# First feed-forward chunk: weight products placed between gate and value matmuls, silu's table loaded ahead of the second halves, three dummy matmuls fewer in q's last groups

## Chip, cores and metric

One core of one Trainium2 chip. The metric is the device time of one execution in microseconds. The profile's span (first to last instruction) is about 2 us shorter than that time. For the runs of the four jobs below it is known for each execution, to 0.1 us, with the mean granted TensorE clock (the share of the full clock that the core was given).

## The reference

```python
# q, k, v: [4, 6016, 256] float32; tau = 1
qn = q / (norm(q, axis=1) + 1e-6);  kn = k / (norm(k, axis=1) + 1e-6)
a = softmax(kn.transpose(0, 2, 1) @ qn / tau, axis=-1)      # [4, 256, 256]
x = (v @ a).reshape(24064, 256)
g = x @ w_gate                                              # [256, 1536]
out = (g * sigmoid(g)) * (x @ w_val) @ w_out
```

## The kernel before

It folds the attention matrix into the feed-forward weights once per batch ("weight products": exp-logits times w_gate and w_val, in 12 units) and then streams v through gate, value and output matmuls. A chunk is 512 rows of v; a step of a chunk is 128 of the 1536 feed-forward columns; a unit is a product for 512 columns, which for the first four units is made in two halves (lo, hi). For batch 0 nothing hides the start: q and k are loaded and reduced first. While q's last four groups come in, the kernel puts dummy matmuls (`keep_warm`) between the real ones.

```python
    for g, which, gl in order:               # k's groups, then q's (NQ = 9; sizes 8,8,8,8,4,4,4,2,1)
        ...
        sqs = [first_square(0, t, which, on_dve=(t % 2 == 1)) for t in ts]   # ScalarE / VectorE
        if which == 0:
            for t in ts:
                gemm1_pair(0, t)             # q'k products, L168/L173
            if g == G_COLS:                  # G_COLS = NQ - 4
                first_cols(0)
            if g in (NQ - 4, NQ - 3):
                keep_warm(1)                 # dummy, L404
        for t, sq in zip(ts, sqs):           # column sums, L218, from G_COLS on
            ...
            if G_COLS <= g < NQ - 2:
                keep_warm(NQ - 2 - g)
    first_softmax(0)   # root, exp, row sums; first halves of units 0-3; then:
        #   for u in range(2): wp_unit(b, u, psum_o, "o", hi)   (unit 0 on ScalarE, 1 on VectorE)
        #   nc.scalar.preload_act_table(ACT.Silu)
    ...
        for f in range(FH):                  # steps of a chunk; gi == 0 is the first chunk
            g_ps, v_ps, mv = gv_matmuls(b, ci, f)
            us = range(2 * f + 2, min(2 * f + 4, len(wp_units))) if gi == 0 else ()
            part = hi if f == 0 else full
            for u in us[:1]:
                wp_unit(0, u, psum_o, "o", part, on_dve=True)
            silu = gv_silu(g_ps, mv)
            for u in us[1:]:
                wp_unit(0, u, psum_o, "o", part, on_dve=(f == 0))
            gv_product(f, sv, silu, v_ps, mv)
            ...
```

Of the kernel before, what the change touches and what calls it, by code (L numbers as in the profile page):

```python
# [13 lines left out]
ACT = mybir.ActivationFunctionType  # L14
# [4 lines left out]
def kernel(  # L19
# [11 lines left out]
    nc = tc.nc  # L31
# [42 lines left out]
    psum_o = ctx.enter_context(tc.tile_pool(name="psum_o", bufs=2, space=bass.MemoryType.PSUM))  # L74
    psum_kq = ctx.enter_context(tc.tile_pool(name="psum_kq", bufs=1, space=bass.MemoryType.PSUM))
    psum_m = ctx.enter_context(tc.tile_pool(name="psum_m", bufs=1, space=bass.MemoryType.PSUM))
# [76 lines left out]
    def evacuate_first_v(h):  # L153
        nc.vector.tensor_copy(vt_ready[(0, 0)][:, h, :], state["vt_ps"][:, h, :])
# [43 lines left out]
    def first_row_copy(b):  # L198
        row = work.tile([1, C], FP32, tag="row")
        nc.vector.tensor_copy(row, state[b, "ss", 0][0:1, :])  # L200
        state[b, "row"] = row
# [21 lines left out]
    def first_root(dst, src):  # L223
        nc.scalar.activation(dst, src, ACT.Ln)
        nc.scalar.activation(dst, dst, ACT.Exp, scale=0.5)
# [11 lines left out]
    def first_softmax(b):  # L237
        kq, ink = state[b, "kq"], state[b, "ink"]
        inq = work.tile([P, CH], FP32, tag="inq")
        first_root(inq, state[b, "cols"])  # L240
        s_f = work.tile([P, CH, C], FP32, tag="s_f")
        nc.vector.tensor_mul(s_f[:, 0, :], kq[:, 0, :], ink)
        nc.vector.tensor_scalar_add(inq, in0=inq, scalar1=1e-6)
        nc.vector.reciprocal(inq, inq)
        if inv_tau != 1.0:
            nc.vector.tensor_scalar_mul(inq, in0=inq, scalar1=inv_tau)
        nc.vector.tensor_mul(s_f[:, 1, :], kq[:, 1, :], ink)
        rs = psum_m.tile([P, CH], FP32, tag="misc")
        keep_warm(1)
        row_eps(rs)  # L250
        transpose_first_v()
        keep_warm(2)
        for h in range(CH):
            evacuate_first_v(h)
        exT = attn.tile([P, CH, C], BF16, tag="exT")
        state[b, "exT"] = exT
        for jh in range(CH):
            nc.scalar.activation(exT[:, jh, :], s_f[:, jh, :], ACT.Exp,
                                 scale=inq[:, jh:jh + 1])


        def row_sum(jh):
            for ih in range(CH):
                nc.tensor.matmul(rs[:, ih:ih + 1], exT[:, jh, ih * P:(ih + 1) * P],
                                 ones_bf[:, 0:1], start=False,
                                 stop=(jh == CH - 1), skip_group_check=True)

        units = []
        for u in range(2 * CH):
            unit_ps = psum_gv.tile([P, HW], FP32, tag="gv"[u % 2])  # L270
            units.append(unit_ps)
        row_sum(0)
        wp_matmul(b, 0, 0, units[0], lo)
        wp_matmul(b, 1, 0, units[1], lo)
        wp_matmul(b, 2, 0, units[2], lo)
        row_sum(1)
        finish_rs(b, rs)
        for u, jh in ((0, 1), (1, 1), (2, 1), (3, 0), (3, 1)):
            wp_matmul(b, u, jh, units[u], lo)
        for u in range(4):  # L280
            wp_evacuate(b, u, units[u], lo, u % 2 == 1)
        for u in range(2):
            wp_unit(b, u, psum_o, "o", hi)
        nc.scalar.preload_act_table(ACT.Silu)

    def norm_acc(b, t):
        q_sb, k_sb = qk_tiles[b]
# [88 lines left out]
    def row_eps(rs):  # L376

        nc.tensor.matmul(rs, ones_f[0:1, :], eps[0:1, :], start=True, stop=False,
                         skip_group_check=True)
# [21 lines left out]
    def keep_warm(n):  # L401
        ps = psum_o.tile([P, 2, C], FP32, tag="o")
        for _ in range(n):
            nc.tensor.matmul(ps, ones_bf, warm_bf, start=True, stop=True)  # L404

    wp_units = [(wc, w, ih) for wc in range(NWC) for w in range(2) for ih in range(CH)]

    HW = WP // 2
    full, lo, hi = slice(0, WP), slice(0, HW), slice(HW, WP)
# [8 lines left out]
    def wp_evacuate(b, u, ps, part, on_dve):  # L418
        wc, w, ih = wp_units[u]
        scale = state[b, "smr"][:, ih:ih + 1]  # L420
        cols = slice(wc * WP + part.start, wc * WP + part.stop)
        dst = state[b, "W"][w][:, ih, cols]
        if on_dve:
            nc.vector.tensor_scalar_mul(dst, in0=ps, scalar1=scale)
        else:
            nc.scalar.activation(dst, ps, ACT.Copy, scale=scale)  # L426

    def wp_unit(b, u, pool=psum_m, tag="misc", part=full, on_dve=None):

        ps = pool.tile([P, part.stop - part.start], FP32, tag=tag)  # L430
        for jh in range(CH):
            wp_matmul(b, u, jh, ps, part)
        wp_evacuate(b, u, ps, part, u % 2 == 1 if on_dve is None else on_dve)

    def gv_matmuls(b, ci, f):
        cs, cm = chunks[ci]
        mv = cm * P
        Wg, Wv = state[b, "W"]
        vT = vt_ready[(b, ci)]
        fs = slice(f * P, (f + 1) * P)  # L440
        g_ps = psum_gv.tile([P, CS * P], FP32, tag="g")
        v_ps = psum_gv.tile([P, CS * P], FP32, tag="v")
        for dst, W in ((g_ps, Wg), (v_ps, Wv)):
            for kk in range(CH):
                nc.tensor.matmul(dst[:, :mv], W[:, kk, fs], vT[:, kk, :mv],  # L445
                                 start=(kk == 0), stop=(kk == CH - 1))
        return g_ps, v_ps, mv
# [189 lines left out]
    NG, NQ = len(kgroups), len(qgroups)  # L637
# [15 lines left out]
    G_COLS = NQ - 4  # L653
    T_COLS = qgroups[G_COLS][0] // 2
    for g, which, gl in order:
        gs, gm = gl[g]
        ts = list(range(gs // 2, (gs + gm + 1) // 2))
        if which == 0 and g == NQ - 1:
            continue
        if which == 0 and g == NQ - 2:  # L660

            gs, gm = gl[g + 1]
            ts += range(gs // 2, (gs + gm + 1) // 2)
        if which == 0 and g == G_COLS:
            first_row_copy(0)
        sqs = [first_square(0, t, which, on_dve=(t % 2 == 1)) for t in ts]
        if which == 0:
            for t in ts:
                gemm1_pair(0, t)
            if g == G_COLS:  # L670
                first_cols(0)
            if g in (NQ - 4, NQ - 3):
                keep_warm(1)
        for t, sq in zip(ts, sqs):
            if which == 0 and g >= G_COLS:
                first_col_sums(0, t, sq)
            else:
                first_row_sums(0, t, which, sq, (T_COLS if which == 0 else NP) - 1)
        if which == 0:
            if g == 0:  # L680
                first_norm_k(0)
                nc.vector.tensor_copy(ident, identf)
            elif g <= 4:
                first_inv_k(0, g - 1)

            if G_COLS <= g < NQ - 2:
                keep_warm(NQ - 2 - g)
    first_softmax(0)


    later = {}

    def at_step(n, what, *args):
        later.setdefault(n, []).append((what, args))

    prev = None
    for gi, (b, ci) in enumerate(allc):
        sv = svpool.tile([P, FH, CS * P], BF16, tag="sv")
        for f in range(FH):
            now = gi * FH + f  # L700
            g_ps, v_ps, mv = gv_matmuls(b, ci, f)


            us = range(2 * f + 2, min(2 * f + 4, len(wp_units))) if gi == 0 else ()
            part = hi if f == 0 else full
            for u in us[:1]:
                wp_unit(0, u, psum_o, "o", part, on_dve=True)
            silu = gv_silu(g_ps, mv)
            for u in us[1:]:
                wp_unit(0, u, psum_o, "o", part, on_dve=(f == 0))  # L710
            gv_product(f, sv, silu, v_ps, mv)
            if prev is not None:
                prev.step()
            if b + 1 < B:
                background(b + 1, ci * FH + f)
            if f == 0 and gi + VT_AHEAD < len(allc):
                load_v(*allc[gi + VT_AHEAD])
                at_step(now + 6, transpose_v, *allc[gi + VT_AHEAD])
            for what, args in later.pop(now, ()):
                what(*args)  # L720
        if gi < len(allc) - 2:
            prev = OutColumns(b, ci, sv)
            n0 = (gi + 1) * FH
            for h in range(CH):
                n = n0 + FH // CH * (h + 1) - 1
                at_step(n, prev.copy, h)
                at_step(n + 2, prev.spill, h)
                at_step(n + 5, prev.transpose, h)
            at_step(n0 + 22, prev.store)
        else:  # L730
            prev = OutStage(b, ci, sv)
# [35 lines left out]
```

## Time and profile before

| | before |
|---|---|
| time, median of the first 3 runs | 811.31 us (810.81 to 812.25) |
| span of the profiled run | 809.0 us |
| TensorE busy | 98% |
| first gate matmul of chunk 1 | 38.05 us |
| first output matmul of chunk 2 | 53.28 us |

The prediction shows the lines on which it rests. "Row copy" is VectorE's copy of q's row sums (31.37 us): up to there the two kernels do the same, so its position is the scatter of a run's start. "First output matmul of chunk 2" lies behind everything that the change touches. The stretch between them, 21.91 us, is what the change can shorten.

### The profile page before, as it was taken

The numbers are of one execution on the slowest core, as the hardware profiler recorded it, in microseconds if no ns is written. First come the engines' busy times: TensorE is split into PE (matmuls) and PEld (weight loads), VectorE is DVE, ScalarE is ACT, GpSimd is POOL, SyncE is SP. The second block draws the span as 40 slices with busy tenths as digits, with TensorE's granted clock in tenths as the row PEclk, the third lists the DMA queues.
The fourth block names the chain that finished last, engine by engine and source line by source line (L and its number), as shares of the span: only waits on it lengthen the run. The fifth ranks groups of instructions, "written<-read, shape, count | busy, mean of one in ns | idle before, by whom it ended". The sixth has DMA issues, their size and how long they took to land.

```text
span 809.0 us, 11969 instructions
## 1 busy us (share of the span) xinstructions
PE 793.5 (98%) x3979; PEld 385.0 (48%) x3979; DVE 550.3 (68%) x841; ACT 454.7 (56%) x803; POOL 256.7 (32%) x314
## 2 busy tenths in 40 slices
PE   4999999999999999999999999999999999999998
PEld 2644444444454444444454444444445444444446
DVE  4777887668667888667666787756866665666654
ACT  4566666555556666555555666655555555555553
POOL 4415888422104786422000777720100000000000
PEclk9999999999999999999999999999999999999999
DMA  9995999799887885889997787468647656565443
GB/s 90 144 154 93 172 157 178 138 123 170 168 152 141 143 140 124 168 71 197 142 147 168 140 156 152 120 133 150 146 105 138 132 138 134 140 127 133 113 119 98
DMA packets 202077, 112.34 MB, mean 139 GB/s; under 512 B 149808, under 2 KB 188848, under 8 KB 201264
## 3 DMA queue, kind: packets, MB, share of 16 engines
q1 hardware_dynamic: 183968, 84.51, 44.8%
q0 software_dynamic: 17904, 27.01, 31.6%
q8 instruction: 31, 0.51, 0.3%
q14 instruction: 30, 0.25, 0.1%
q10 hardware_dynamic: 144, 0.07, 0.0%
HBM read 79.04 MB, written 60.43 MB: 172 GB/s over the span
## 4 chain that ended last, share of the span: by engine, by line
PE 96%; DMA 3%; issue 0%; DVE 0%; POOL 0%; POOLq 0%
PE g_ps L445 30%; PE v_ps L445 30%; PE o_new L486 29%; PE ps L414 2%; DMA q_sb<-in_q_dram 2%; PE kq_new L168 2%; PE o_new L539 1%; DMA k_sb<-in_k_dram 1%; PE ps L404 0%; PE last_ps L563 0%; PE ss_new L195 0%; PE kq_new L173 0%; PE unit_ps L414 0%; PE cs L324 0%; POOL k_sb L111 0%
## 5 line engine op out<-in xcount | busy, mean ns | idle before, releaser
L455 DVE TENSOR_TENSOR sv<-silu,v_ps 128x512 bf16<-128x512 bf16 (+1 forms) x576 | 387.3, 673 | 217.2 <-ACT silu L451 215.8
L451 ACT ACTIVATE silu<-g_ps 128x512 bf16<-128x512 f32 (+1 forms) x576 | 339.3, 589 | 294.3 <-PE g_ps L445 261.3
L445 PE MATMUL g_ps<-vT,Wg 128*128 128x512 bf16 (+1 forms) x1128 | 330.7, 375 | 0.0
L445 PE MATMUL v_ps<-vT,Wv 128*128 128x512 bf16 (+1 forms) x1128 | 330.3, 374 | 0.0
L486 PE MATMUL o_new<-sv,w_out_sb 128*128 128x512 bf16 (+1 forms) x1104 | 324.6, 376 | 0.0
L445 PEld LDWEIGHTS <-Wv 128*128 128x128 bf16 x1152 | 112.7, 98 | 130.7 <-ACT Wv L426 0.2
L300 POOL TENSOR_TENSOR acc_new<-acc_new,sq 128x512 f32<-128x512 f32 x135 | 156.2, 1157 | 55.2 <-DVE sq L290 40.7
L486 PEld LDWEIGHTS <-w_out_sb 128*128 128x128 bf16 x1104 | 108.0, 98 | 126.5
L445 PEld LDWEIGHTS <-Wg 128*128 128x128 bf16 x1152 | 109.6, 98 | 122.2
L126 POOL DMA_DIRECT2D vb_new<-in_v_dram x47 | 24.2, 514 | 257.6 <-DMA vT<-vb_new 256.7
L496 DVE COPY pl<-o_new 128x512 uint16<-128x512 uint16 (+1 forms) x92 | 62.6, 680 | 17.2 <-ACT pl L495 16.8
L290 DVE TENSOR_TENSOR sq<-q_sb 128x512 bf16<-128x512 fp8e5 x72 | 66.0, 916 | 0.0
L495 ACT COPY pl<-o_new 128x512 uint16<-128x512 uint16 (+1 forms) x92 | 53.1, 578 | 18.9 <-PE o_new L486 18.7
L291 ACT ACTIVATE sq<-k_sb 128x512 bf16<-128x512 fp8e5 x72 | 44.2, 614 | 0.0
L168 PE MATMUL kq_new<-k_sb,q_sb 128*128 128x512 fp8e5 x184 | 34.8, 313 | 1.6 <-DMA q_sb<-in_q_dram 1.6
L111 POOL DMA_DIRECT2D q_sb<-in_q_dram x45 | 25.3, 563 | 11.9 <-DMA k_sb<-in_k_dram 10.0
L168 PEld LDWEIGHTS <-q_sb 128*128 128x256 fp8e5 x184 | 22.1, 136 | 10.2 <-DMA q_sb<-in_q_dram 2.8
L195 PE MATMUL ss_new<-sq,ones_bf 128*128 128x256 bf16 x83 | 14.8, 336 | 10.9 <-ACT sq L185 10.9
L359 POOL TENSOR_SCALAR den<-th 128x512 f32<-128x512 f32 x3 | 1.8, 615 | 73.1 <-ACT th L358 73.1
L111 POOL DMA_DIRECT2D k_sb<-in_k_dram x42 | 23.0, 548 | 3.1 <-DVE sq L290 1.7
L295 POOL TENSOR_TENSOR acc_new<-sq 128x512 f32<-128x512 bf16 x3 | 3.5, 1151 | 42.5 <-DVE sq L290 42.5
L195 PEld LDWEIGHTS <-ones_bf 128*128 128x128 bf16 x83 | 9.4, 119 | 14.9 <-issue 10.8
(96 smaller groups left out, 214.4 us busy)
## 6 DMA issues: line engine op xcount, KB each, us to landing
rows<-pl SPq DMA_DIRECT2D x86, 256.0 KB, 2.8
out_dram<-ot_new SPq DMA_DIRECT2D x43, 512.0 KB, 3.9
vb_new<-in_v_dram POOLq DMA_DIRECT2D x43, 256.0 KB, 4.9
q_sb<-in_q_dram POOLq DMA_DIRECT2D x36, 128.0 KB, 6.1
k_sb<-in_k_dram POOLq DMA_DIRECT2D x33, 128.0 KB, 7.1
ot_new<-rows SPq DMA_TRANSPOSE x92, 3.7
k_sb<-in_k_dram POOLq DMA_DIRECT2D x5, 256.0 KB, 9.1
rows<-pl SPq DMA_DIRECT2D x6, 192.0 KB, 2.5
```

The source lines that it names most:

```text
L111: nc.gpsimd.dma_start(out=dst[:, gs:gs + gm, :], in_=src[b].rearrange("(p s) c -> p s c", s=NS)[:, gs:gs + gm, :])
L168: nc.tensor.matmul(kq[:, jh, :], q_sb[:, ps:ps + 2, js], k_sb[:, ps:ps + 2, :], start=(t == 0 and jh == 0), stop=last, perf_mode=DR, skip_ ...
L195: nc.tensor.matmul(state[b, "ss", which], ones_bf, sq[:, s, :], start=(t == 0 and s == 0), stop=(t == t_last and s == pm - 1))
L290: nc.vector.tensor_mul(sq[:, :pm, 0, :], q_sb[:, ps:ps + pm, :], q_sb[:, ps:ps + pm, :])
L291: nc.scalar.activation(sq[:, :pm, 1, :], k_sb[:, ps:ps + pm, :], ACT.Square)
L300: nc.gpsimd.tensor_tensor(out=acc, in0=acc, in1=sq[:, s, :, :], op=ALU.add)
L445: nc.tensor.matmul(dst[:, :mv], W[:, kk, fs], vT[:, kk, :mv], start=(kk == 0), stop=(kk == CH - 1))
L451: nc.scalar.activation(silu[:, :mv], g_ps[:, :mv], ACT.Silu)
L455: nc.vector.tensor_mul(sv[:, f, :mv], silu[:, :mv], v_ps[:, :mv])
L486: nc.tensor.matmul(self.o_ps[h][:, :self.mv], w_out_sb[:, f, h * P:(h + 1) * P], self.sv[:, f, :self.mv], start=(f == 0), stop=(f == FH - 1))
L495: nc.scalar.copy(pl[:, 0, :self.mv], halves[:, 0, :self.mv])
L496: nc.vector.tensor_copy(pl[:, 1, :self.mv], halves[:, 1, :self.mv])
```

## The change

Intent: let real weight products fill TensorE where waits were expected, load silu's table earlier, and drop dummies that stand on the chain. The diff is cut: the lines of the old order that it removes stand in the excerpt above.

```diff
-        for u in range(2):
-            wp_unit(b, u, psum_o, "o", hi)
         nc.scalar.preload_act_table(ACT.Silu)
+        for u in range(2):
+            wp_unit(b, u, psum_o, "o", hi, on_dve=True)
...  (gv_matmuls calls between() just ahead of the value matmuls)
-            if g in (NQ - 4, NQ - 3):
+            if g == NQ - 4:
                 keep_warm(1)
...
-            if G_COLS <= g < NQ - 2:
-                keep_warm(NQ - 2 - g)
+            if g == G_COLS:
+                keep_warm(1)
...
+            us = range(2 * f, 2 * f + 2) if gi == 0 and 2 <= f < len(wp_units) // 2 else ()
+            if us:
+                g_ps, v_ps, mv = gv_matmuls(
+                    b, ci, f, lambda: wp_unit(0, us[0], psum_o, "o", on_dve=True))
+            else:
+                g_ps, v_ps, mv = gv_matmuls(b, ci, f)
+            if gi == 0 and f == 0:
+                wp_unit(0, 2, psum_o, "o", hi, on_dve=True)
+                wp_unit(0, 3, psum_m, "misc", hi, on_dve=True)
             silu = gv_silu(g_ps, mv)
+            if us:
+                wp_unit(0, us[1], psum_o, "o", on_dve=False)
```

More of the change, by code (lines that the diff above doesn't have):

```diff
@@ L281, in first_softmax @@
             wp_evacuate(b, u, units[u], lo, u % 2 == 1)
+        nc.scalar.preload_act_table(ACT.Silu)
         for u in range(2):
-            wp_unit(b, u, psum_o, "o", hi)
-        nc.scalar.preload_act_table(ACT.Silu)
+            wp_unit(b, u, psum_o, "o", hi, on_dve=True)
     def norm_acc(b, t):
@@ L433, in wp_unit, with gv_matmuls @@
         wp_evacuate(b, u, ps, part, u % 2 == 1 if on_dve is None else on_dve)
-    def gv_matmuls(b, ci, f):
+    def gv_matmuls(b, ci, f, between=None):
         cs, cm = chunks[ci]
@@ L443, in gv_matmuls @@
         for dst, W in ((g_ps, Wg), (v_ps, Wv)):
+            if between is not None and dst is v_ps:
+                between()
             for kk in range(CH):
@@ L700 @@
             now = gi * FH + f
-            g_ps, v_ps, mv = gv_matmuls(b, ci, f)
-            us = range(2 * f + 2, min(2 * f + 4, len(wp_units))) if gi == 0 else ()
-            part = hi if f == 0 else full
-            for u in us[:1]:
-                wp_unit(0, u, psum_o, "o", part, on_dve=True)
+            us = range(2 * f, 2 * f + 2) if gi == 0 and 2 <= f < len(wp_units) // 2 else ()
[7 more added lines that the diff above has]
+                wp_unit(0, 3, psum_m, "misc", hi, on_dve=True)
             silu = gv_silu(g_ps, mv)
-            for u in us[1:]:
-                wp_unit(0, u, psum_o, "o", part, on_dve=(f == 0))
+            if us:
+                wp_unit(0, us[1], psum_o, "o", on_dve=False)
             gv_product(f, sv, silu, v_ps, mv)
```

## The prediction

> **What bounds the kernel now.** I first read the page: the busy shares and the chain that ended last.
>
> ```profile
> PE 793.5 (98%) x3979; PEld 385.0 (48%) x3979; DVE 550.3 (68%) x841; ACT 454.7 (56%) x803; POOL 256.7 (32%) x314
> PE 96%; DMA 3%; issue 0%; DVE 0%; POOL 0%; POOLq 0%
> ```
>
> The first line gives busy time, share and instruction count; the second is the chain by engine. TensorE is the chain for 96% of the span. Since a busy TensorE need not be at its peak, I also took the start-to-start distance of all matmuls after 42 us. A 128x512 matmul follows the one before by 0.216 us (39.352, 39.568, 39.784 in the trace). In the 767 us from 42.06 on, only one distance exceeds 0.216 by more than 0.03 without an fp8 pair product being there (0.282 at 196.9). So that long stretch has no slack: it takes up no delay and gives none back. The change can only move the moment at which it starts. The whole question is the first 47 us, which I read next, as the chain in time (start, us, what).
>
> ```profile
> 31.84 0.60 PE cols L208 x4
> 32.44 0.32 PE ps L404
> 32.76 0.18 PE cols L218 x8
> 32.94 0.45 PE ps L404 x2
> 33.40 0.44 PE kq_new L168 x4
> 33.83 0.23 PE ps L404
> 34.06 0.18 PE cols L218 x8
> 34.24 0.24 PE ps L404
> 34.48 0.22 PE kq_new L168 x2
> 34.70 0.23 PE kq_new L173 x2
> 34.93 0.13 PE cols L218 x6
> ```
>
> Here L404 is a dummy matmul (keep_warm), whose result nobody reads. Dummies are links of the chain themselves: the real products behind them had their data. The last four groups of q are issued at 14.32, 16.76, 18.88 and 21.34 and take 16.7, 15.8, 14.3 and 12.3 us to land, so they are there at 31.0, 32.6, 33.2 and 33.6 us, but their products start at 31.1, 33.2, 34.3 and 34.5. In this stage TensorE runs late because of its dummies.
>
> Last, the timelines of ScalarE, VectorE and TensorE at the start of the first chunk (start, us, engine, line).
>
> ```profile
> 38.24 0.48 ACT L426 ACTIVATE Wg<-ps,smr 128x256 bf16<-128x256 f32 x1
> 38.74 1.28 ACT L284 ACT_TABLE_LOAD   x1
> 40.03 1.09 ACT L451 ACTIVATE silu<-g_ps 128x512 bf16<-128x512 f32 x2
> ```
> ```profile
> 41.27 0.74 DVE L424 TENSOR_SCALAR Wg<-ps,smr 128x512 bf16<-128x512 f32 x1
> ```
> ```profile
> 41.51 0.59 PE L445 MATMUL v_ps<-vT_new,Wv 128*128 128x512 bf16 x2
> 42.06 1.02 PE L414 MATMUL ps<-w_val_sb,exT 128*128 128x512 bf16 x4
> ```
>
> From 38.05 on TensorE is dense but for one place: the last value matmul of step 2 starts at 41.726, so the next product was due at 41.942, and it starts at 42.064. It waits 0.12 us for VectorE to empty the PSUM tile of the product two before (41.27 + 0.74 = 42.01, plus 0.05 for the semaphore).
>
> **What the Trainium skill says.** "TensorE: Matmul & The Clock Gate", section "Wait — 56ns, not 53.3ns?", gives 215.7 ns between warm matmuls of 512 columns; the trace agrees (0.2155). Its section "What's actually happening" says that the clock falls to half after an idle window and that activity releases it. The trace shows it: from 17.3 to 20.7 us the granted clock is 0.50, after a stretch (13.8 to 17.3) in which TensorE was busy for 1.35 of 3.4 us; the stretches after it, with 2.7 us and more, all have 1.00. "ScalarE: Activation LUTs", section "What ACT_TABLE_LOAD costs", states about 1283 ns for the load plus about 1380 ns of drain; the trace has the 1.28 us, but the first silu starts 0.01 us after it, so I count no drain.
>
> **The change, part by part.**
>
> *Dummies.* The order of instructions on TensorE has three pairs of weight load and dummy fewer: the second of two before the third-last group of q, and one on each side of that group's column sums.
> 1. Without the second dummy at 33.02, the pair products of that group start 0.216 earlier (their landing, 32.57, is past). The group begins at 33.02 rather than 33.24.
> 2. Without the dummy at 33.67, the column sums start when the four products end, 33.46 rather than 33.90: shift 0.44. They need the squares: ScalarE's end at 33.31, VectorE's at 33.35. Just in time.
> 3. The dummy at 34.10 hid a weight load: the next fp8 weights load behind it. Without it, that load (0.11 exposed) stands alone, so it brings 0.216 - 0.11 = 0.11 more, and adding the small steps between them I get 0.57 in all. Products now at 33.75 and 33.96 (landings 33.2, 33.6), last sums at 34.2 (squares: 33.95 and 34.18). All fit.
>
> So the sums' end moves from 34.92 to about 34.35. What follows (root, reciprocal, exp, row sums, first weight products) is a chain of PE, ScalarE and VectorE that moves along, unless a load is late. From issue plus time to landing: v's first chunk 23.86 + 11.0 = 34.9 (needed at 34.96), first gate columns 26.29 + 9.2 = 35.5 (needed 36.1), first value columns 28.71 + 7.5 = 36.2 (needed 36.3), second gate columns 29.97 + 6.9 = 36.87 (needed 36.93); what is needed is the time in the trace of before less 0.57. Four loads land 0.03 to 0.6 us ahead. So 0.57 is nearly the most that removing dummies could ever bring.
>
> *Table load.* ScalarE no longer evacuates the second half of unit 0 (0.48), and loads silu's table right after the first halves: 37.80 to 39.08 with the shift. First silu 39.09 to 39.68, against 40.03 to 40.62; so 0.95 earlier, of which 0.57 is the shift.
>
> *Order in the first chunk.* Step 1 loses its two products (four matmuls of 512 columns, 0.86 us of TensorE), and each later product stands a step later. The matmuls are the same, in another order. The first gate matmul starts at 38.05 - 0.57 = 37.48; five blocks of 0.43 (gate and value of step 0, two half products, gate and value of step 1) come before step 2's gate matmuls, so these are due at 39.64, but need the PSUM tile that the first silu reads until 39.68, plus 0.05: a new wait of 0.10. The product for columns 512 to 1023 follows at 40.17; its weights land at 40.1 (33.51 + 6.6), again just in time. That is what the place between gate and value is for: in the old order, shifted by 0.57, it would have been due at 39.64 and waited 0.5 us. The next product wanting VectorE's evacuation is due at 41.90; VectorE empties its tile at about 41.69 (40.94 + 0.75), so the old wait of 0.12 goes. I followed the later products in the same way to step 5 and found the closest at 0.1 us of margin.
>
> Sum: -0.57 (dummies) - 0.12 (old wait) + 0.10 (new wait) = -0.59 us. 811.31 - 0.59 = 810.7.
>
> **The rivals.**
> - *The loads take the dummies' place.* The weights' landings don't depend on TensorE. For: margins of 0.03 to 0.1 at four of them, so a load that is 0.3 late gives 0.3 back. Against: all land before they are needed in this trace. If it happens, 811.0 to 811.3.
> - *The clock falls.* Fewer dummies could make a window idle enough for half clock. For: the 17.3 us event. Against: the windows that would be touched had 3.35 and 3.40 us of work of 3.4, and the dummies leave a stretch that gets shorter, not emptier; the sums follow one another. If it happened, 3.4 us at half speed would cost about 1.7 us: 812.5.
> - *ScalarE or VectorE becomes the bound of steps 0 to 3.* VectorE takes one more half evacuation (they follow one another at 0.40 us), and the silu wait of 0.10 could be 0.3 if the table load began later. If so, 811.0.
> - *Placing products between gate and value saves several waits.* Against: there was one wait, of 0.12.
>
> **Range and chances.** Even stripping all idle time of TensorE between 28 and 47 us (under 2 us) would be 0.25% of the time, so a gain over 2% (16 us) is out of reach, and the largest loss I can name is about 2 us. What sets the range is scatter: the three runs before spread over 1.4 us, more than the effect. Around 810.7 I take -0.9 and +0.9: 809.8 to 811.6. Faster 0.005, same 0.99, slower 0.005.
>
> **What would show it right or wrong.** Right: TensorE's last column sums end near 34.3 rather than 34.9; the first gate matmul starts near 37.5 rather than 38.05; the table load starts near 37.8; the step-2 gate matmul waits about 0.1 us for silu; no distance above 0.22 us among the 512-wide matmuls from there to step 6; the first output matmul of the second chunk starts near 52.7 instead of 53.28, and everything after keeps that lead. Wrong: a wait of TensorE for a q, v or weight load at 33 to 40 us; a granted clock of 0.5 in a window after 30 us; or a lead at 53 us that is lost later, which would mean that the long stretch had slack that I did not see.

## The result, and the profile after

After: 810.55 us, median of 4 runs (810.38 to 811.19); before, in the same rounds, 811.78 (810.81 to 812.36). The ratio is 0.9987, 95% interval 0.997 to 1.0005: the same, by the 2% measure. Here and below a ratio is the mean time of one kernel's fast runs over that of the other's of the same rounds, so not quite the ratio of the medians. The time fell inside the predicted range (809.8 to 811.6), at 0.15 us from the predicted 810.7. But the two medians differ by 1.2 us, twice what was predicted, and the trace of after shows a smaller gain, 0.48 us at the first output matmul of chunk 2 (52.80 against 53.28), of which 0.17 is only an earlier start (row copy at 31.20). So neither number can be taken as it stands.

The chain in time of the kernel after, where the prediction showed that of before (start, us, what):

```profile
31.67 0.60 PE cols L208 x4
...
32.43 0.35 PE cols L218 x8
32.79 0.04 issue
32.83 0.64 ACT sq L185
33.47 0.05 issue
33.52 0.35 PE cols L218 x8
33.87 0.27 PE kq_new L168 x2
34.14 0.23 PE kq_new L173 x2
34.38 0.20 PE cols L218 x6
```

L404 is a dummy, L218 are the column sums, L168 and L173 the products of q and k. Three dummies are gone, and ScalarE's square of q (L185), which the column sums need, stands in the chain in their place: q's group 6 landed at 32.73 in this run, 0.16 later than in the trace of before, though the run started 0.17 earlier. TensorE now waits for data. Then ScalarE and TensorE at the start of the first chunk:

```profile
37.84 1.28 ACT L282 ACT_TABLE_LOAD   x1
39.13 1.09 ACT L453 ACTIVATE silu<-g_ps 128x512 bf16<-128x512 f32 x2
```
```profile
39.29 0.59 PE L447 MATMUL v_ps<-vT_new,Wv 128*128 128x512 bf16 x2
39.78 0.59 PE L447 MATMUL g_ps<-vT_new,Wg 128*128 128x512 bf16 x2
40.29 0.59 PE L414 MATMUL ps<-w_gate_sb,exT 128*128 128x512 bf16 x2
40.72 0.59 PE L447 MATMUL v_ps<-vT_new,Wv 128*128 128x512 bf16 x2
41.15 0.59 PE L414 MATMUL ps<-w_gate_sb,exT 128*128 128x512 bf16 x2
```

Two matmuls of 512 columns take 0.43 us at full clock. From 39.29 to 39.78 is 0.49: 0.06 of wait for silu (predicted 0.10). From 39.78 to 40.29 is 0.51: 0.08 of wait for the second block of gate weights, which landed at 40.25. After that every block follows at 0.43, and the wait of 0.12 that before had at 41.94 is gone.

### The profile page after: what moved, and what is told of

The parts are those of the page before. It is cut to its first block, busy times and chain, and to the rows that moved or that the text cites. A ratio compares the mean times of both kernels' runs of the same rounds, so it can differ in the third digit from the quotient of the medians.

```text
span 808.5 us, 11893 instructions
## 1 busy us (share of the span) xinstructions
PE 788.9 (98%) x3902; PEld 384.6 (48%) x3976; DVE 550.3 (68%) x842; ACT 454.4 (56%) x802; POOL 256.7 (32%) x314
## 4 chain that ended last, share of the span: by engine, by line
PE 95%; DMA 3%; issue 1%; ACT 0%; DVE 0%; POOL 0%; POOLq 0%
PE g_ps L447 30%; PE v_ps L447 30%; PE o_new L488 29%; PE ps L414 2%; DMA q_sb<-in_q_dram 2%; PE kq_new L168 2%; PE o_new L541 1%; DMA k_sb<-in_k_dram 1%; ACT silu L453 0%; PE last_ps L565 0%; PE ss_new L195 0%; PE unit_ps L414 0%; PE kq_new L173 0%; PE cols L218 0%; ACT pl L497 0%
## 5 line engine op out<-in xcount | busy, mean ns | idle before, releaser
L447 PE MATMUL v_ps<-vT,Wv 128*128 128x512 bf16 (+1 forms) x1107 | 325.9, 374 | 1.2
L447 PE MATMUL g_ps<-vT,Wg 128*128 128x512 bf16 (+1 forms) x1105 | 325.7, 375 | 1.2
L488 PE MATMUL o_new<-sv,w_out_sb 128*128 128x512 bf16 (+1 forms) x1079 | 319.2, 375 | 1.3
L497 ACT COPY pl<-o_new 128x512 uint16<-128x512 uint16 (+1 forms) x92 | 53.1, 577 | 18.9 <-PE o_new L488 17.9
L168 PE MATMUL kq_new<-k_sb,q_sb 128*128 128x512 fp8e5 x184 | 34.5, 312 | 1.7 <-DMA q_sb<-in_q_dram 1.7
L168 PEld LDWEIGHTS <-q_sb 128*128 128x256 fp8e5 x184 | 22.0, 136 | 10.0 <-DMA q_sb<-in_q_dram 2.9
L295 POOL TENSOR_TENSOR acc_new<-sq 128x512 f32<-128x512 bf16 x3 | 3.5, 1153 | 40.9 <-DVE sq L290 40.9
```

The lines of the kernel that those rows point to most:

```text
L168: nc.tensor.matmul(kq[:, jh, :], q_sb[:, ps:ps + 2, js], k_sb[:, ps:ps + 2, :], start=(t == 0 and jh == 0), stop=last, perf_mode=DR, skip_ ...
L447: nc.tensor.matmul(dst[:, :mv], W[:, kk, fs], vT[:, kk, :mv], start=(kk == 0), stop=(kk == CH - 1))
L488: nc.tensor.matmul(self.o_ps[h][:, :self.mv], w_out_sb[:, f, h * P:(h + 1) * P], self.sv[:, f, :self.mv], start=(f == 0), stop=(f == FH - 1))
L497: nc.scalar.copy(pl[:, 0, :self.mv], halves[:, 0, :self.mv])
```

## The experiments

Each job also timed the kernel before beside its kernels. I first give the jobs (they ran on four chips), then count all spans together. "Distance" is from the row copy to the first output matmul of chunk 2, in the one trace of each run.

### First job: the change again, and its parts

**again**: the changed kernel, unaltered.

> The changed kernel unaltered, for a better interval and a second trace. Measure: the distance from VectorE's copy of the q row sums (up to which both kernels are the same) to the first output matmul of the second chunk: 53.28 - 31.37 = 21.91 us before, 52.80 - 31.20 = 21.60 us in the one trace of after. My theory (dummies and order together bring a few tenths of a microsecond, the rest of the measured 1.2 us between the medians is scatter of start and of loads): distance 21.3 to 21.7, timed 0.3 to 0.7 us faster than before. Rival (the trace missed something and the true gain is 1.2 us): over 1.0 us faster with an interval that excludes 0.6.

Measured: 810.51 us (810.17 to 811.24), ratio 0.9989 (0.9977 to 1.0002). The distance was 22.12, longer than before's 21.91, which neither theory had expected. The timeline of TensorE shows why:

```profile
30.75 0.61 PE L195 MATMUL ss_new<-sq,ones_bf 128*128 128x256 bf16 x4
32.24 0.65 PE L168 MATMUL kq_new<-k_sb,q_sb 128*128 128x512 fp8e5 x4 [0.88 <-DMA q_sb<-in_q_dram]
32.82 0.60 PE L208 MATMUL cols<-ones_f,row 1*128 1x1 f32 x4
```

The products of q's group 5 start at 32.24, after 0.88 us of idle time ended by q's load; in the trace of before they start at 31.09. A load here counts its semaphore up by 16, and the products started 0.05 after the sixteenth count: fifteen had come by 31.02, as usual, and the last came at 32.19. The spans of this job fall into two groups: before 808.9 to 809.0 (4 runs) and 809.8 to 810.0 (4 runs), with one at 811.2; again 808.2 to 808.5 (3) and 809.2 to 809.3 (2), its traced run being one of the latter. I call them early and late runs.

**dummies_only**: before, with the dummies edit alone.

```diff
-            if g in (NQ - 4, NQ - 3):
+            if g == NQ - 4:
                 keep_warm(1)
-            if G_COLS <= g < NQ - 2:
-                keep_warm(NQ - 2 - g)
+            if g == G_COLS:
+                keep_warm(1)
```

> The kernel before with only the three dummies taken out. My theory: the first gate matmul moves 0.3 to 0.57 us ahead, but the product of the second block of gate columns is then due at about 39.65 and waits for its weights, which land at 40.1 to 40.25, so nearly all is given back: distance (row copy to first output matmul of chunk 2) 21.7 to 22.0 against 21.91 of before, time within 0.2 us of before. Rival (the dummies are the whole gain and the order is worth nothing): distance 21.3 to 21.6, time 0.3 to 0.6 faster.

Measured: 811.23 us, ratio 0.9994 (0.998 to 1.0007); spans 808.8, 808.8, 808.9, 808.9 and 809.3. The traced run is the last, and late: its distance, 22.17, is that of again's late run (22.12). So in the one late run the dummies alone bring 0.7 (809.3 against 810.0), as the rival said and more (three dummies at 0.22 are 0.65); in early ones 0.15, as my theory said, though no early run was traced to show the wait.

**order_only**: the changed kernel with before's two `keep_warm` conditions put back.

> The changed kernel with its dummies put back as before: order, table load and VectorE's evacuation alone. My theory: the old wait of 0.12 before the value product goes and a wait of about 0.09 for silu comes, so it is worth 0.03 us: distance 21.8 to 21.95, time within 0.2 us of before. Rival (order and table are the gain): distance 21.3 to 21.6.

Measured: 811.91 us, ratio 1.0002 (0.9989 to 1.0014); spans 808.8 (one early run), 809.9, 809.9, 809.9 and 810.2. In late runs the order is worth nothing that the spans show; the one early run is 0.2 below before's 809.0. The trace (late, and with every load after group 5 some 0.4 us later than usual) can't be compared by its distance, 23.16.

**late_table**: after, with unit 0's second half on ScalarE and the table load behind it.

```diff
-        nc.scalar.preload_act_table(ACT.Silu)
         for u in range(2):
-            wp_unit(b, u, psum_o, "o", hi, on_dve=True)
+            wp_unit(b, u, psum_o, "o", hi)
+        nc.scalar.preload_act_table(ACT.Silu)
```

> The changed kernel with unit 0's second half back on ScalarE and silu's table loaded after it. My theory: the first silu ends about 0.4 us later, step 2's gate matmuls wait about 0.5 instead of 0.06 to 0.1 us for the PSUM tile that it reads, and the lead shrinks by about 0.4 us: distance 21.9 to 22.1. Rival (the silu wait is covered by the wait for the second block of gate weights, which ends at 40.3 in any case): the lead shrinks by 0.1 or less.

Measured: 811.56 us, ratio 1.0006 (0.9989 to 1.0023); spans 808.6, 809.2, 809.6 and 812.4, the last (814.56 us) with a mean clock of 0.994 and no trace. The traced run is early, span 808.6 and distance 21.67, against 21.60 and 21.46 in the two early traces of after. The distance missed my range and is near the rival's. But the wait for silu did grow,

```profile
39.05 0.59 PE L447 MATMUL v_ps<-vT_new,Wv 128*128 128x512 bf16 x2
39.94 0.59 PE L447 MATMUL g_ps<-vT_new,Wg 128*128 128x512 bf16 x2 [0.29 <-ACT silu L453]
40.37 0.59 PE L414 MATMUL ps<-w_gate_sb,exT 128*128 128x512 bf16 x2
```

from 39.05 to 39.94 is 0.89, so 0.46 of wait. The product behind it starts at 40.37, where after had it at 40.29; but the two runs are not alike. In this one the weights had landed at 40.02, not 40.25. Without the wait the product was due at 39.91 and could have started at some 40.06 (0.04 after the landing, as in after), so by this estimate the later table load cost 0.3 us here. The distances agree: ScalarE's root comes 0.11 sooner after the row copy than in after_third (3.17 against 3.28), yet the distance is 0.21 longer. My 0.4 was nearer than the rival's 0.1 or less.

### Second job: before's own scatter, and attempts at more

**before_again**: the kernel before, unaltered.

> The kernel before, unaltered. The runs so far have spans in two groups: before 808.9 to 809.0 and 809.8 to 810.0; after 808.2 to 808.6 and 809.2 to 809.3; and the traces of the later group show one of the 16 completion counts of q's group 5 (the fourth-last) arriving 1.2 us after the other fifteen (32.2 against 31.0 us). My theory: an execution is early or late by this straggler, and the change gains 0.5 in early runs and 0.65 to 0.7 in late ones, so the difference of 1.2 between the medians mixes groups. Expect two groups at 809.0 and 809.9 again, and in the trace the first gate matmul at 38.05 with q's group 5 at 31.0, or at about 39.1 with it at 32.2. Rival (the scatter is not from q's group 5): a run of the later group whose group 5 landed at 31.0.

Measured: 811.66 us, ratio to itself 1.0002; spans 808.9, 809.0, 809.2 and 810.1, 810.2. The traced run is early. By luck it matches the first trace of after load for load: row copy at 31.20 in both, group 6 landed at 32.74 and 32.73, the second gate weights at 40.26 and 40.25. Its chain does not run through the dummies at all:

```profile
16.59 16.15 DMA q_sb<-in_q_dram
32.74 0.28 issue
33.02 0.54 POOL vb_new L126
33.56 0.12 issue
33.68 6.58 DMA w_gate_sb<-in_moe_w_gate_dram
40.27 0.04 issue
40.31 1.04 PE ps L414 x4
```

In this trace GpSimd issues v's next chunk and then the second block of gate weights only when a load of q has landed, and the weight product waits for that load. TensorE was ready earlier:

```profile
39.50 0.59 PE L445 MATMUL v_ps<-vT_new,Wv 128*128 128x512 bf16 x2
40.31 1.04 PE L414 MATMUL ps<-w_gate_sb,exT 128*128 128x512 bf16 x4 [0.21 <-DMA w_gate_sb<-in_moe_w_gate_dram]
```

From 39.50 to 40.31 is 0.81, so 0.38 us of wait. That is the rival of my prediction, "the loads take the dummies' place", and before has it already in this run, with all its dummies.

**no_dummies**: after, without its last two dummies in q's groups (both `keep_warm` conditions taken out).

> The changed kernel without the two dummies that it kept in q's last groups. My theory: in an early run the squares of q's group 6 (ready about 33.35 to 33.5) set the pace, so nothing more is to be had: span 808.3 to 808.5, as after. In a late run TensorE is the chain from 32.2 on, and two dummies less bring 0.3 to 0.43: span 808.8 to 808.95 instead of 809.25. Granted clock 1.00 from 24 us on. Rival 1 (dummies hold the clock): a window of 0.5 after 30 us, span 809.5 or more. Rival 2 (dummies always cost 0.216 each): 0.4 faster in both groups.

Measured: 810.78 us, ratio 0.9999 (0.9986 to 1.0012); spans 808.3, 808.5, 808.8 and 810.2, 810.3. The 808.8 is the traced run: it is late, with distance 21.83 against again's 22.12, so two dummies are worth 0.3 in a late run by the distance and 0.45 by the span, as expected; 808.3 and 808.5 are no faster than after's early runs, against rival 2. The traced run kept its clock from 24 us to the last matmul. But two runs are 1.5 us longer, at a mean clock of 0.995 and 0.993. Rival 1 could not be dismissed.

**weights_first**: after, with the second block of gate and value weights issued ahead of v's second chunk.

```diff
+    load_w(WP, 2 * WP)
     load_v(*allc[1])
     transpose_v(*allc[1])
-    for wc in range(1, NWC):
+    for wc in range(2, NWC):
         load_w(wc * WP, (wc + 1) * WP)
```

> The changed kernel with the second block of gate and value weights loaded before v's second chunk. My theory: the weights land about 0.8 us earlier, so in early runs the wait of 0.08 before the second block's product goes: span 808.4 against 808.5; in late runs no difference. The transposes of v's second chunk start later and still land before 52 us. Rival (they land after it is needed at 51.9): a wait of the second chunk's gate matmul, time longer by more than 0.3.

Measured: 816.37 us, ratio 1.0084 (1.0045 to 1.0123). The rival was right, and by far more than the 0.3 that it named:

```profile
51.43 0.59 PE L447 MATMUL v_ps<-vT_new,Wv 128*128 128x512 bf16 x2
55.98 1.04 PE L447 MATMUL g_ps<-vT,Wg 128*128 128x512 bf16 x2 [3.96 <-DMA vT<-vb_new]
56.81 1.06 PE L447 MATMUL v_ps<-vT,Wv 128*128 128x512 bf16 x2
```

The transposing load of v's second chunk was issued at 41.55 instead of 39.10 and took 14.4 us instead of 10.1. TensorE stood for 4 us, and then ran at half clock for two windows (55.1 to 61.9 us): the value pair starts 0.83 us after the gate pair, not 0.43. One run took 827.62 us, 12 more than the fastest; it has no trace.

**both**: no_dummies and weights_first together.

> Both of these edits. My theory: spans 808.3 to 808.45 in early runs, 808.8 to 808.95 in late ones; if the weights' edit does harm, that of the other alone is the better version.

Measured: 816.07 us, ratio 1.0071 (1.0045 to 1.0097). As a kernel it fails like weights_first, but its trace, of the slowest run (823.30 us), bears on another question. Busy time by stretch (the columns are the stretch, its length, PE, PEld, DVE, ACT and POOL busy with counts, granted clock, DMA share, GB/s):

```profile
31.20:34.61 3.41, 3.08 (x40) 2.38 (x39) 2.53 (x6) 1.89 (x5) 2.48 (x4) 1.00 1.23 161
34.61:38.03 3.42, 3.42 (x23) 2.48 (x24) 1.74 (x8) 1.38 (x4) 3.13 (x6) 0.53 1.36 201
```

Before the wait for the late transposes, the clock fell to half from 34.8 to 38.2 us. That is rival 1 of no_dummies, though this kernel also has the other edit; no_dummies_2 below has not.

### Third job: is one dummy enough?

**one_dummy**: after, without the `keep_warm(1)` behind the column sums of group 5.

> The changed kernel with one of its two remaining dummies taken out (the one behind the column sums of q's group 5). My theory: early runs (group 5 landed near 31.0) unchanged at 808.3 to 808.6; late runs 0.2 shorter, 809.05 instead of 809.25. The question is the clock: without both dummies two runs of five had a mean granted clock of 0.995 and 0.993 and were 1.5 us longer. If one dummy is enough to hold it, no run here is over 809.5; if not, some run is near 810 with a clock of 0.995 or less.

Measured: 810.80 us, ratio 0.9989 (0.9977 to 1.0001); spans 808.4, 808.5, 808.5, 809.1, 810.6 and 812.1. The traced run is the last, and late (group 5 landed at 32.39). It was at half clock from 34.1 to 40.9 us, and reached chunk 2's first output matmul at 56.37:

```profile
30.60:34.06 3.46, 2.25 (x24) 1.63 (x23) 2.30 (x5) 1.23 (x2) 1.37 (x3) 1.00 1.18 146
34.06:37.50 3.44, 3.44 (x31) 2.50 (x29) 1.49 (x5) 1.27 (x4) 3.23 (x5) 0.50 1.33 206
37.50:40.89 3.39, 3.39 (x23) 2.34 (x21) 1.43 (x5) 1.37 (x4) 2.15 (x4) 0.50 1.21 200
```

The 810.6 has a mean clock of 1.00 and no trace; its cause stays open.

**no_dummies_2**: no_dummies once more.

> The kernel without any dummy in q's last groups once more, to count the runs with a lower clock. If the dummies hold the clock, again one to three runs of five near 810.2 with a mean granted clock of 0.995 or less (one half-clock window more is 3.41 / 2 / 809 = 0.002), and the others at 808.3 to 808.5 and 808.8; if the two were chance, none.

Measured: 811.07 us, ratio 0.9993 (0.998 to 1.0007); spans 808.4, 808.4, 808.8, 809.4, 809.6 and 811.8, the last two with a clock of 0.994. The 809.6 is the traced run: group 5 landed at 30.8, an early run, and from 35.0 to 38.45 the clock was 0.50:

```profile
31.60:35.04 3.44, 3.21 (x40) 2.47 (x41) 2.28 (x6) 1.63 (x4) 2.17 (x4) 1.00 1.28 173
35.04:38.45 3.41, 3.41 (x23) 2.36 (x22) 1.93 (x7) 1.61 (x4) 3.30 (x5) 0.50 1.26 206
```

**before_third**: the kernel before a third time.

> The kernel before a third time, for a trace of its later group. Theory: if group 5 of q lands near 32.2, the trace has the first gate matmul at 38.9 to 39.2 and no wait for the second block of gate weights before its product; if near 31.0, the first gate matmul is at 37.7 to 38.1 and the wait for these weights is 0 to 0.4. Spans 808.9 to 809.2 and 809.8 to 810.2.

Measured: 812.10 us, ratio to itself 1.0003; spans 808.9, 809.0, 809.9, 810.0, 810.1 and 811.4. The traced run was early again, with the first gate matmul at 37.97, no wait for the weights and the wait of 0.12 at 41.86. A late run of before itself was never traced.

### Fourth job

**after_third**: the changed kernel a third time.

> The changed kernel a third time. So far 9 runs of it: 6 at 808.2 to 808.6, 3 at 809.2 to 809.3, none longer. Theory: two groups at 808.5 and 809.25. The question is the clock: the versions with one dummy or none have had half-clock windows after 34 us (two traces) and runs at 809.6 to 812.1; before has 4 runs of 42 at 811.2 to 811.6. If the changed kernel's two dummies hold the clock as well as before's five, at most one of these runs is above 809.6; if it shares the weakness, two or more are.

Measured: 811.18 us, ratio 0.9992 (0.9978 to 1.0005); spans 808.1, 808.4 and 809.2, 809.3, 809.4. None is above 809.6. The traced run is early, distance 21.46, and its granted clock is 1.00 from 18.9 us to the tail.

### All spans together

| kernel | early runs | late runs | longer |
|---|---|---|---|
| before (51 runs of the four jobs) | 25: 808.8 to 809.2, median 809.0 | 22: 809.6 to 810.2, median 810.0 | 4: 811.2 to 811.6 |
| after (14) | 8: 808.1 to 808.6, median 808.45 | 6: 809.2 to 809.4, median 809.25 | 0 |
| dummies_only (5) | 4: 808.8 to 808.9 | 1: 809.3 | 0 |
| order_only (5) | 1: 808.8 | 3: 809.9, 1: 810.2 | 0 |

In 14 traces group 5 of q landed at 30.8 to 31.0 in nine and at 32.2 to 32.4 in five. The traced runs of before, after, dummies_only and order_only all fit the columns; the assignment of untraced runs goes by their span alone. Like against like, the change gains 0.55 us in early runs and 0.75 in late ones. The mean times over all these runs, 811.80 and 810.75 us, differ by 1.06. Of this, 0.84 is in the spans and 0.22 outside them: time less span is 1.94 to 2.01 us in all 14 runs of after, but over 2.2 (up to 2.55) in 26 of before's 51. The other versions with the new order and the early table load stay at 2.03 or less in all 34 runs; late_table has 2.13 to 2.16, and dummies_only over 2.4 in two of five. No trace covers this time, so what makes it stays open. What the spans have beyond 0.55 to 0.75 is the mix: before has four longer runs and 25 early ones of 51, after no longer run and 8 early ones of 14, and these runs do not tell whether that is more than chance.

## Why the prediction was right

**What bounds the kernel.** Right. No stretch after chunk 1 gave back or took up anything: the lead of 0.48 us at 53 us was still there when the last matmuls began (804.47 and 803.98).

**Dummies, 0.57.** The mechanism was right; the size holds only for the loads of one trace. I worked it out with group 6 landing 1.20 us after the row copy. Measured from the row copy to ScalarE's root (which follows the last column sums; 3.73, 3.72 and 3.73 us in the three traces of before), the early runs of the changed order gained 0.56 with group 6 at 1.31 (late_table), 0.45 at 1.40 (after_third) and 0.31 at 1.52 (after). "Just in time" in step 2 was the weak point: later by a tenth, and the squares set the pace. In after another 0.07 went to the load of the first value columns, which landed at 36.34: their product, due at 36.31, started at 36.38. That is the prediction's rival of the loads in small, and one of its signs of being wrong (a wait for a load at 33 to 40 us); it had given this load a margin of 0.1. (Its phrase "0.03 to 0.1 at four of them" does not fit its own list, where the first gate columns have 0.6.) In late runs TensorE is the chain, and dummies_only gains 0.7 in the one such run.

**Old wait, 0.12.** The step that was incomplete. In the trace that I had, before's first wait was VectorE's, 0.12. In before_again it is the load of the second gate weights, 0.38. I saw that load as a danger to the new order ("would have waited 0.5 us"), and not that before meets it too when the loads land later after the row copy (this one 9.07 us after it, against 8.72 in the first trace).

**New wait, 0.10.** Right: 0.06, 0.09 and 0.06 in the three traces of after. A wait of 0.08 for the weights came on top (39.78 to 40.29 above; the prediction had it start at 40.17, just in time), so its sign of being right, no distance above 0.22, did not come out. Without the early table load the wait for silu was 0.46 (late_table).

**The sum, 0.59.** Near what early runs gain (0.55), but by luck, because two errors cancel: in the matched pair of before_again and after, 0.21 came from the dummies by the first gate matmul (37.77 to 37.56, both by the positions of their neighbours, as this matmul's record is missing in both traces) and 0.38 from not standing in front of the weights, less 0.06 and 0.08: 0.45, where 53.27 - 52.80 = 0.47 is measured. In early runs the dummies alone bring 0.15 (four runs) and the order alone 0.2 (one run), together 0.55. Why is worked out, not traced. With the dummies gone but the old order, TensorE would reach the second gate weights sooner and wait there longer. What the order is worth alone depends on when these weights land: with the loads of before_again I estimate about 0.3 (the wait of 0.38 less one of 0.1 for silu), with those of the first trace the 0.03 that I had expected of order_only.

**The clock.** Right for this change as far as seen: its three traces have no half-clock window between 24 us and the last matmul, and none of its 14 runs is above 809.4. That its two dummies always hold the clock is not shown: late_table has the same two, and one of its four runs was at 812.4 with a mean clock of 0.994. With one dummy less (one_dummy), or two (no_dummies_2, both), three traces have half-clock windows after 34 us. I had argued from the busy share of the window. That was a bad gauge: in no_dummies_2 the window before the fall had 3.21 us of 3.44 busy, more than after's 3.10 of 3.40, which kept its clock, as did no_dummies' trace with 2.44 of 3.42. Many of these are one-column matmuls, whose records last 0.16 us although they start 0.025 apart. What the clock does count is not settled here.

**Scatter.** I gave the range by the three runs' spread and did not know what it was made of. In the traces it is mostly q's group 5, with one of 16 completion counts 1.2 to 1.6 us late; that the untraced late runs have the same cause is inferred from their spans. The timed medians (1.2 apart) may mix early and late runs. Why that one count is late stays open. The time outside the spans (0.22 of the difference of the means) I had not considered at all.

No version tried beats the change for certain: no_dummies and one_dummy are quicker by 0 to 0.45 us when the clock holds, and 1 to 3.6 us slower when it does not.

## What to carry to other kernels

When an effect is smaller than the scatter of the runs, find out what the scatter is made of, and compare runs of the same kind; here, in the traces, a single late completion count parted them. Before crediting an edit with what it removes from the chain, list what lands or finishes just behind it: the gain ends at the next arrival, and a second edit that moves the consumer of that arrival can decide whether the gain is kept. When two traces are compared, first see whether their loads landed alike: late_table looked nearly harmless because its weights had come sooner. Filler matmuls cost nearly their full time here where TensorE was the chain (0.7 for three), but count whether the clock survives without them over many runs, not one.

## What the Trainium skill lacked or had wrong

- "DMA: Bandwidth & Descriptors", section "Why a DMA increments its semaphore by 16 and not by 1", says that only the full 16 means that all has landed; it does not say how far apart the 16 can be. Here fifteen of group 5's counts came within 0.8 us and the last 1.2 to 1.6 us after them, in 5 of 14 traces.
- "TensorE: Matmul & The Clock Gate", section "Why this matters for your kernels", asks for no idle gaps over about 3 us. In no_dummies_2 the clock fell at 35.04 although no two matmuls in the 3.4 us before started more than 0.37 us apart. The page gives no measure of how much short idles or one-column matmuls count.
- "ScalarE: Activation LUTs", section "What ACT_TABLE_LOAD costs": the load took 1.28 us, as stated; the 1.38 us of drain did not show, as silu started 0.01 us after the load in before and in after.
